# Twelve expert slots in one straight plan, with the rare groups and the fallbacks behind one test each at the end

## The chip, the core and the metric

The kernel runs on one core of a Trainium2 chip. The time of a run is the device time of one execution in microseconds. PE is the matrix engine (TensorE; PEld is its queue of weight loads), DVE is VectorE, ACT is ScalarE, POOL is GpSimd, and SP starts most of the transfers. Each engine works through its instructions in the order in which they were written for it; semaphores make one wait for another.

## The reference

There are 3072 tokens (4 sequences of 768), 384 numbers wide (8 heads of 48). Three layers follow one another.

```python
# 1. a linear recurrence per head, complex decay, real output
a_n = a * min(|a|, 0.999) / (|a| + 1e-6)
S[t] = a_n[t, :, None] * S[t-1] + k[t, :, None] * v[t, None, :]      # 48 x 48, complex
y[t] = q[t] @ S[t].real
# 2. a dense layer with a rational function
h = x @ w_in                                      # 3072 x 384 @ 384 x 2048
g = (a0 + a1 h + a2 h^2 + a3 h^3) / (1 + |b0| |h| + |b1| h^2 + 1e-6)
x = g @ w_out                                     # 2048 x 384
# 3. a mixture: each token goes to one of 8 experts
logits = normalize(x) @ normalize(emb).T / tau
e = argmax(logits); gate = softmax(logits)[e]
out = gate * (relu(x @ w1[e]) @ w2[e])            # 384 x 1024, 1024 x 384
```

All of it is fp32. A product is made of three matmuls of rounded parts (x_hi w_hi + x_lo w_hi + x_hi w_lo), so every operand is split on ACT, DVE or POOL into a high part (a copy, L967) and a low part (a difference, L1387 for expert weights, L1366 for tokens).

## The kernel before

**Order.** Nearly nothing is written in the order in which it runs. A stage hands its operations to a `Plan` with the engines that may do them, their costs, what they read and write and a due time; `Plan.emit` then writes them out one by one by a greedy rule with prices for each engine. Attention has one plan; the rational layer, the routing and the first eight slots share one (knobs `MOE`); each branch behind that has one of its own (knobs `TAIL`). A branch ends a plan: all engines read a flag (L153, L1631) and branch (L154, L1653, L1703).

**Attention** leaves its result in `xT`, transposed; its last pieces come by transfers on SP (L660). Two checks on DVE set `bad`: decays that the fast recurrence can't take, and coefficients that the fast rational function can't take. The branch at L154 holds a slow recurrence and a slow rational layer, which also fills `safe`; with these data it is not taken.

**The rational layer** takes 8 blocks of 384 tokens through 8 units of 256 inner columns: up products (L1003), the function on ACT and DVE (L1026 to L1038), down products (L1048). `route` follows a block: its rows are copied, replaced by rows of `safe` under a condition (`mend`, L1075, 24 transfers on SP), the expert is chosen, tokens are counted (L1103 to L1108) and listed for each expert (L1115, scatters on POOL).

**The mixture** takes slots of 256 tokens of one expert. A slot is gathered on POOL (`gather`, L1343), transposed on PE (L1361), split (L1366), its gates are copied (L1368); its weights are loaded by SP into one raw buffer per matrix (`load`, L1327), and split (`slot_split`). `work` then does four quarters: up products, relu (gh on L1421, gl on L1422; those of quarters 2 and 3 are gh, gl2e, gh3e, gl3e), down products (L1433). The two halves of the slot are scaled by the gate (L1438) and scattered to the output on POOL (L1391). In a slot that ends a stretch (`end`), all up products stand first, then the down products of the first half of the tokens, then those of the second. What slots there are is computed by DVE as chains of small operations on one partition (L978). Tokens left over by full slots go into remainders of 32 (`mini`, L1548 to L1569) beside slots 4 to 7, and into halves of 128 behind the last branch (`halves`).

Eight slots are certain for any routing (`LAST` = 8). For more there are three branches of 4, 2 and 1 slots (L1653), then the branch for halves (L1703). The straight part and each branch also prepare what the next branch needs: slot `hi` wholly (`ready`: gather, load, transposes, splits), of slot `hi + 1` the gather and the load. With these data there are 12 full slots, so the branch of four is taken and the others are not. Where a body ends, POOL has a semaphore instruction that waits for all its transfers (INC_SWDGE_SEM in the rows).

Of the kernel before, what the change touches and what calls it, by code (L numbers as in the profile page):

```python
# [9 lines left out]
F32 = mybir.dt.float32  # L10
# [29 lines left out]
NSURE = (NT - E * HALF) // SLOT - NEARLY  # L40
NTAIL = 7
# [40 lines left out]
def constants():  # L82
# [20 lines left out]
    c[:, C_J:C_J + NSLOT] = list(range(NSURE + 4)) + [NSURE, NSURE + 1, NSURE, NSURE + 1]  # L103
# [15 lines left out]
def tile_recurrence_rational_moe(tc, q, k, v, a_re, a_im, w_in, w_out, ca, cb, emb, tau, w1, w2, cst_d, out):  # L119
# [3 lines left out]
    with ExitStack() as top:  # L123
# [18 lines left out]
        with ExitStack() as moe1:  # L142
            xtp = moe1.enter_context(tc.tile_pool(name="xtp", bufs=1))
            xT = xtp.tile([P, KT, NT], F32, name="xT")
            wfp = moe1.enter_context(tc.tile_pool(name="wfp", bufs=1))
            hold = moe1.enter_context(tc.tile_pool(name="hold", bufs=1))
# [4 lines left out]
            with ExitStack() as att:  # L151
                attention(tc, att, q, k, v, a_re, a_im, w_in, w_out, emb, cst, cst_d, cc, misc, ident, hold, xT, bad, idl, x2d, coef, parts, xs)
            flag = lambda i: nc.values_load(bad[0:1, i:i + 1], min_val=0, max_val=1) != 0  # L153
            with tc.If(flag(0)):  # L154
                with tc.If(flag(1)):
                    sequential_attention(tc, q, k, v, a_re, a_im, cst, cc, ident, dram, xT, coef)
                    for kk in range(KT):
                        xs.hi(nc.scalar, 0, kk)
                        xs.lo(nc.gpsimd, 0, kk)
# [253 lines left out]
def attention(tc, ctx, q, k, v, a_re, a_im, w_in, w_out, emb, cst, cst_d, cc, misc, ident, hold, xT, bad, idl, x2d, coef, parts, xs):  # L413
# [290 lines left out]
    A.preload_act_table_set("trig_and_small")  # L704
    for t in vraw + sraw:
        G.memset(t[:, DM:W], 0.0)
    V.memset(rows[0], 0.0)
    V.memset(gap[:, 2:4, :], -2.0)
    load_a(0, 0)
    load(cst[:, 0:C_ID], cst_d[:, 0:C_ID], ["misc"], 0.1)  # L710
    ext = raw[0].rearrange("p f w -> p (f w)").bitcast(F32)[:, 0:NX * P]
    load(ext, cst_d[:, C_X:C_X + NX * P], [("raw", 0)], 0.92)
    add(("V", 0.41), lambda e: V.tensor_copy(trir, ext.rearrange("p (n m) -> p n m", n=NX)), r=[("raw", 0)], w=["trir"])
    load_a(0, 1)
    load(cst[:, C_ID:], cst_d[:, C_ID:C_N], ["cst"], 1.2)
# [20 lines left out]
    for g in range(NG):  # L736
        u = g // NB
        if g % NB == 0:
            if u:
                for i in range(NB):  # L740
                    load_a(u, i)
        load_q(g)
        if g == 0:
            prep(0, 0)
            prep(0, 1)
        elif g % NB == 0:
            if u in HALVED:
                prep(u, 0)
                prep(u, 1)
            else:  # L750
                prep(u)
        phases(g)
# [12 lines left out]
        chunk(g)  # L765
# [5 lines left out]
    m, mm = new("m", [P, 1])[0], new("mm", [1, 1])[0]  # L771
    top = new("top", [P, 3])[0]

    def worst(i):
        def fn(e):
            V.tensor_reduce(out=top[:, i:i + 1], in_=rows[i], axis=AX.X, op=ALU.max)
            if i:
                V.tensor_scalar(top[:, i:i + 1], top[:, i:i + 1], (-FAR_SQ, MAG_LOW)[i - 1], None, op0=ALU.add)
        add(("V", 0.16), fn, r=[("gap", n, g) for n in range(2) for g in range(NG)], w=[("top", i)])

    for i in range(3):
        worst(i)
    add(("V", 0.1), lambda e: V.tensor_reduce(out=m, in_=top, axis=AX.X, op=ALU.max), r=[("top", i) for i in range(3)], w=["m"])
    add(("T", 0.1), lambda e: T.transpose(pb("pm")[0:1, :P], m, ident), r=["m"], w=["pm"], take=("B", "pm"))
    add(("V", 0.2), lambda e: V.tensor_reduce(out=mm, in_=pb("pm")[0:1, :P], axis=AX.X, op=ALU.max), r=["pm"], w=["mm"], give="pm")
    add(("V", 0.1), lambda e: V.tensor_scalar(bad[0:1, 1:2], mm, 0.0, None, op0=ALU.is_gt), r=["mm"], w=["bad"], due=end)
    add(("V", 0.1), lambda e: V.tensor_copy(bad[0:1, 2:3], coef.flag[0:1, :]), r=["coef"], w=["bad"], due=end)
    add(("V", 0.1), lambda e: V.tensor_tensor(out=bad[0:1, 0:1], in0=bad[0:1, 1:2], in1=bad[0:1, 2:3], op=ALU.max), w=["bad"], due=end)
# [7 lines left out]
    seen = [("xT", i, r) for i in (0, 1) for r in {r for h in range(H) for r in (h * D, (h * D // P + 1) * P)}]  # L796
    for kk in range(KT):
        qs, ks = ([(n, i) for i in range(NQ)] if not kk else [] for n in ("q", "k"))
        add(("A", 0.41), lambda e, kk=kk: xs.hi(A, 0, kk), r=seen + (["x0"] if kk else []), w=qs + ks + ([] if kk else ["x0"]) + [("xh", kk)], due=end)
        add(("G", 0.96), lambda e, kk=kk: xs.lo(G, 0, kk), r=seen + [("xh", kk)], w=[("xl", kk)], due=end)  # L800
# [120 lines left out]
def mixture(tc, ctx, cst, cc, misc, ident, cp, hold, wfp, parts, xs, xT, cnt, idl, x2d, w1, w2, out, coef, bad, safe):  # L921
# [133 lines left out]
    rows, kept = [], []  # L1055
# [7 lines left out]
    def route(b):  # L1063
# [8 lines left out]
        def mend(t):  # L1072
            if not kept:
                kept.append(val(bad[0:1, 2:3], 1))
            SY.dma_start(rows[t], safe[b * BLK + t * P:b * BLK + (t + 1) * P, :], cond=kept[0])  # L1075

# [85 lines left out]
    tail = row("tail", 8, I32)  # L1162
# [34 lines left out]
    ns, ce, nf, tf = row("ns", E), row("ce", E), row("nf", E), row("tf", 4)  # L1197
# [13 lines left out]
    def slot_table(V):  # L1211
# [9 lines left out]
        rest = tf[:, 3:4]  # L1221
        V.tensor_scalar(rest, ce[:, E - 1:E], float(NSURE), None, op0=ALU.subtract)
        groups(V, tf, rest, (4, 2, 1))
        V.tensor_copy(tail[:, 0:3], tf[:, 0:3])
        V.tensor_copy(jb, cst[0:1, C_J:C_J + NSLOT])
        V.tensor_scalar(tf[:, 0:2], tf[:, 0:2], 2.0, None, op0=ALU.mult)
        for n, o in ((0, 4), (0, 4), (1, 6)):
            V.tensor_scalar(jb[:, NSURE + o:], jb[:, NSURE + o:], tf[:, n:n + 1], None, op0=ALU.add)
# [510 lines left out]
```

## Time and profile before

| | us |
|---|---|
| runs (three) | 967.56, 960.59, 961.06; median 961.06 |
| profiled execution | 965.73 |
| its span | 964.0 |
| PE busy in it | 879.6 (91%) |
| DVE, ACT, POOL busy | 747.4, 704.4, 280.8 |

The span is the stretch that the profile records, from the first instruction to the last; the execution is 1.7 us longer. Attention ends near 256 on PE, the rational layer near 690, the straight slots near 860. In the rows below a time in front is microseconds from the span's start, and an arrow in brackets (<-) names what ended the wait before an operation.

### The profile page before, as it was taken

What the parts mean: (1) busy time and instruction counts of PE and PEld (TensorE: products, weight loads), DVE (VectorE), ACT (ScalarE), POOL (GpSimd) and SP (SyncE); (2) the same over time, 40 slices, a digit from 0 to 9 for tenths busy, and PEclk for the clock granted to TensorE, in tenths of its full rate; (3) what the DMA queues carried; (4) which work ended last, traced back from release to release, by engine and by line L of the source; (5) the groups of instructions that cost most, each with busy time, mean ns of one, the idle gap of its engine ahead of it and who ended that gap; (6) DMA issues with size and microseconds to landing.
All of it is one profiled execution on the core that took longest, in us unless ns stands there. A gap on an engine that the chain in (4) does not pass through costs nothing.

```text
span 964.0 us, 17300 instructions
## 1 busy us (share of the span) xinstructions
PE 879.6 (91%) x6125; PEld 835.8 (87%) x6125; DVE 747.4 (78%) x1444; ACT 704.4 (73%) x1133; POOL 280.8 (29%) x213
## 2 busy tenths in 40 slices
PE   2899999989689999999999999999989999999960
PEld 2788897878679999999999999999889888879960
DVE  7989998879799988787978788886986865566250
ACT  7989998969576898888889898978545444345540
POOL 2425444445353110101010010103033234316881
PEclk9999999969889999999999999999999999999985
DMA  9978997764300000000100000105112276631511
GB/s 174 196 171 182 186 186 161 166 142 107 85 1 1 1 1 25 9 18 1 25 1 26 1 25 1 26 1 151 39 27 67 47 217 190 221 118 27 172 39 32
DMA packets 178236, 78.73 MB, mean 82 GB/s; under 512 B 145672, under 2 KB 172184, under 8 KB 178132
## 3 DMA queue, kind: packets, MB, share of 16 engines
q1 hardware_dynamic: 173460, 65.60, 30.1%
q0 software_dynamic: 4672, 11.83, 4.5%
q8 instruction: 55, 0.90, 0.4%
q14 instruction: 49, 0.40, 0.2%
HBM read 105.48 MB, written 9.96 MB: 120 GB/s over the span
## 4 chain that ended last, share of the span: by engine, by line
PE 56%; DVE 6%; ACT 3%; issue 3%; POOL 3%; DMA 0%; POOLq 0%; DVEq 0%; ACTq 0%
PE ph L1003 27%; PE acc L1048 18%; PE acc L1433 8%; POOL wi L1387 1%; DVE xT L978 1%; PE acc L1361 1%; DVE wo L1387 1%; PE ph L1548 1%; DVE sq L1034 1%; DVE u L1036 1%; POOL out_dram L1391 1%; DMA out_dram<-ah,ido 0%; DVE wi L1387 0%; ACT sq L1026 0%; POOL wo L1387 0%
## 5 line engine op out<-in xcount | busy, mean ns | idle before, releaser
L1003 PE MATMUL ph<-xh,wi 128*128 128x384 f32 (+1 forms) x1284 | 305.0, 316 | 10.7 <-DVEq L154 7.6
L1003 PEld LDWEIGHTS ph<-xh,wi 128*128 128x128 f32 x1284 | 223.1, 189 | 14.2 <-issue 10.1
L1048 PE MATMUL acc<-wo,gh 128*128 128x392 f32 x768 | 202.2, 345 | 3.3 <-ACT gh L1037 3.3
L1003 PE MATMUL ph<-xl,wi 128*128 128x384 f32 (+1 forms) x642 | 202.6, 316 | 0.2 <-DVE xl L1366 0.2
L1048 PEld LDWEIGHTS acc<-wo,gh 128*128 128x128 f32 x768 | 141.2, 190 | 3.6 <-ACT gh L1037 3.6
L1048 PE MATMUL acc<-wo,gl 128*128 128x392 f32 x384 | 132.1, 344 | 1.4 <-DVE gl L1038 1.3
L1003 PEld LDWEIGHTS ph<-xl,wi 128*128 128x128 f32 x642 | 121.5, 189 | 0.4 <-DVE xl L1366 0.4
L1115 POOL DMA_INDIRECT idl<-tok,pos x24 | 25.0, 1042 | 304.1 <-DVE pos L1112 152.7
L1048 PEld LDWEIGHTS acc<-wo,gl 128*128 128x128 f32 x384 | 72.9, 190 | 2.4 <-DVE gl L1038 2.3
L1433 PE MATMUL acc<-wo,gh 128*128 128x384 f32 x272 | 71.9, 345 | 0.0
L1421 ACT ACTIVATE gh<-ph 128x512 fp32r<-128x512 f32 x34 | 20.4, 600 | 58.0 <-PE ph L1003 45.6
L1038 DVE TENSOR_TENSOR gl<-u,gh 128x768 fp32r<-128x768 f32 x48 | 46.9, 978 | 19.5 <-PE acc L1048 18.7
L1343 POOL DMA_INDIRECT xT<-x2d,ids x28 | 30.5, 1090 | 103.4 <-DVE oh L1094 43.1
L1026 ACT ACTIVATE sq<-ph,quad 128x768 f32<-128x768 f32 x43 | 38.8, 902 | 26.7 <-PE ph L1003 24.3
L1031 DVE SCALAR_TENSOR_TENSOR u<-u,qtmp,ph 128x768 f32<-128x768 f32 x47 | 47.4, 1009 | 13.2 <-ACT u L1029 12.8
L485 ACT COPY qkT<-bank 96x512 f32<-96x512 f32 x96 | 51.0, 587 | 6.2 <-PE bank L607 5.8
L616 PE MATMUL bank<-qkT 96*128 96x128 f32 x384 | 51.1, 281 | 1.1 <-ACT qkT L485 1.1
L606 PE MATMUL bank<-cst,qf 128*96 128x128 f32 x192 | 49.7, 296 | 2.3 <-ACT qkT L485 2.3
L1034 DVE SCALAR_TENSOR_TENSOR sq<-sq,quad,ah 128x768 f32<-128x768 f32 x43 | 46.2, 1075 | 6.5 <-ACT ah L1033 6.4
L1433 PEld LDWEIGHTS acc<-wo,gh 128*128 128x128 f32 x272 | 48.1, 191 | 2.5 <-issue 1.7
L616 PEld LDWEIGHTS bank<-qkT 96*128 96x128 f32 x384 | 47.5, 195 | 2.5 <-ACT qkT L485 2.3
L1387 DVE TENSOR_TENSOR wo<-xT,wo 128x768 fp32r<-128x768 f32 x41 | 40.8, 1024 | 10.2 <-ACT wo L967 10.1
(308 smaller groups left out, 2195.9 us busy)
## 6 DMA issues: line engine op xcount, KB each, us to landing
xT<-in_moe_w_dram SPq DMA_DIRECT2D x28, 1536.0 KB
mw<-in_moe_w_dram SPq DMA_DIRECT2D x32, 384.0 KB
raw<-in_moe_w_out_dram SPq DMA_DIRECT2D x16, 384.0 KB
raw<-in_moe_w_in_dram SPq DMA_DIRECT2D x16, 384.0 KB
rows<-safe SPq DMA_DIRECT2D x24, 196.0 KB
x2d<-rows SPq DMA_DIRECT2D x24, 192.5 KB
a_re<-in_a_re_dram SPq DMA_DIRECT2D x24, 192.0 KB
a_im<-in_a_im_dram SPq DMA_DIRECT2D x24, 192.0 KB
```

The costliest lines, as they stand in the source:

```text
L485: (A.copy if e == "A" else eng[e].tensor_copy)(o, i)
L606: T.transpose(pv[:, i, 0, :], Q[:, 2 * j + i, :], ident)
L616: T.matmul(pb(b)[:, i * P:(i + 1) * P], O[:, i, 1, :], O[:, i, 0, :], start=True, stop=True)
L1003: T.matmul(o, l, r, start=(n == 0), stop=(n == len(steps) - 1))
L1026: add(("A", 0.81 if many else 0.45), lambda e, c=c, h=h: A.activation(z[:, c], h(), AF.Abs, scale=coef.kb), w=kh + kz_)
L1031: add(("V", 0.93 if many else 0.53), lambda e, c=c, h=h: V.scalar_tensor_tensor(out=w[:, c], in0=w[:, c], scalar=coef.d, in1=h(), op0=ALU. ...
L1034: add(("V", 0.93), lambda e: V.scalar_tensor_tensor(out=z, in0=z, scalar=coef.e, in1=s, op0=ALU.add, op1=ALU.mult), r=ks, w=kz_)
L1038: add(("V", 0.87), lambda e: V.tensor_tensor(out=l, in0=w, in1=g.bitcast(F32), op=ALU.subtract), r=kw + kg, w=kl, lat=0.27)
L1048: T.matmul(o, x[:, j, sl], y("o", i)[:, c], start=(i == 0 and j == 0 and k == 0), stop=(i == NP - 1 and j == 1 and k == 2))
L1343: G.indirect_dma_start(out=xg[i][t], out_offset=None, in_=x2d[0:n, :], in_offset=bass.IndirectOffsetOnAxis(ap=ids[i][:, t:t + 1], axis=0), ...
L1387: add([("V", 0.87)] if lone and k else [("V", 0.87), ("G", 1.76)], lambda e, src=src, v=v, o=o: eng[e].tensor_tensor(out=v(wset(s, q)[o + ...
L1433: T.matmul(o, x[:, j, sl], w[:, c], start=(q == 0 and j == 0 and n == 0), stop=(q == NQ - 1 and j == 1 and n == 2))
```

## The change

`NSURE` goes from 5 to 9, so `LAST` is 12: twelve slots are written in the straight plan, whatever the routing. The groups behind it are of 2 and 1 slots; they and the halves stand together behind one new flag, `tail[8]`, the maximum of the flags of the two groups and of the halves. The branch between attention and mixture is gone. If `bad` is set, a branch at the end of the program holds a second run: the slow recurrence, the slow rational layer and the whole mixture once more. The rows of `safe` are copied in that second run alone, without a condition. `plan_half` (gathers for seven halves in the straight plan) and the preparation of the next branch (`ready`) are gone; of the slot after the last one only the load under a condition stays. The buffers for the weights' parts are numbered anew from slot 8 on, and the last slot, 11, now has the order `end`. The planner's knobs are as they were.

```diff
-NSURE = (NT - E * HALF) // SLOT - NEARLY
-NTAIL = 7
+NSURE = NT // SLOT - NEARLY
+EXTRA = (2, 1)
+NTAIL = sum(EXTRA)
...
-            with tc.If(flag(0)):
-                with tc.If(flag(1)):
-                    sequential_attention(tc, q, k, v, a_re, a_im, cst, cc, ident, dram, xT, coef)
...
-                with tc.If(flag(2)):
-                    plain_rational(tc, coef, parts, xT, safe)
-            mixture(tc, moe1, cst, cc, misc, ident, cp, hold, wfp, parts, xs, xT, cnt, idl, x2d, w1, w2, out, coef, bad, safe)
+            prepare(False)
+            with ExitStack() as first:
+                rare, rest = layers(first, False)
+                with tc.If(nc.values_load(rare, min_val=0, max_val=1) != 0):
+                    rest()
+            with tc.If(nc.values_load(bad[0:1, 0:1], min_val=0, max_val=1) != 0):
+                xs.tiles.clear()
+                prepare(True)
+                sequential_attention(tc, q, k, v, a_re, a_im, cst, cc, ident, dram, xT, coef)
...
+                plain_rational(tc, coef, parts, xT, safe)
+                with ExitStack() as second:
+                    layers(second, True)[1]()
...
-            add(("S", 0.65 if b or t else 2.25), lambda e, t=t: mend(t), w=[("row", t)], lat=1.8)
+            if again:
+                add(("S", 0.65), lambda e, t=t: SY.dma_start(rows[t], safe[b * BLK + t * P:b * BLK + (t + 1) * P, :]), w=[("row", t)], lat=1.8)
...
+        V.tensor_tensor(out=tail[:, 8:9], in0=tail[:, 0:1], in1=tail[:, 1:2], op=ALU.max)
+        V.tensor_tensor(out=tail[:, 8:9], in0=tail[:, 8:9], in1=tail[:, 7:8], op=ALU.max)
...
     def chunk(s, q):
         n = NQ * s + q
-        return n % 6 if NEARLY <= s < LAST else n % 8
+        if s >= LAST:
+            return 2 + n % 6
+        return n % 6 if NEARLY <= s < BESIDE.stop else (n + (2 if s >= BESIDE.stop else 0)) % 8
...
-        work(s)
-        m = s - NEARLY - 1
-        if 0 <= m < NMINI:
+        if s == BESIDE.stop:
+            mini_end()
+        work(s, s == LAST - 1)
+        if s in BESIDE:
+            m = s - BESIDE.start
             mini_load(NHALF + m)
             mini(m, st.start(s) + 5.0)
-        if s == NEARLY + 1:
-            for p in (0, 1, 2, 3, 8, 9, 10):
-                plan_half(p)
-    mini_end()
-    ready(LAST)
-    gather(LAST + 1)
-    load(LAST + 1)
+    load(LAST)
...
-    for n, (lo, hi) in enumerate(((0, 4), (4, 6), (6, 7))):
-        with tc.If(flag(n)):
-            group(LAST + lo, LAST + hi)
...
+    def rest():
+        for n, lo in enumerate((LAST, LAST + EXTRA[0])):
+            with tc.If(flag(n)):
+                group(lo, lo + EXTRA[n])
+        with tc.If(flag(7)):
...
+    return tail[:, 8:9], rest
```

On PE, between the last product of attention (`bank`) and the first up product of the rational layer (`ph`), there stood before:

```order
L634 MATMUL bank_153<-qkT_142,S_138 64x128
L153 TENSOR_LOAD bad
L154 COMPARE_AND_BRANCH
L153 TENSOR_LOAD bad
L155 COMPARE_AND_BRANCH
...
L915 MATMUL pr_acc_3011<-wfo_171,pr_w 128x392
L160 UNCONDITIONAL_BRANCH x2
L154 UNCONDITIONAL_BRANCH
L1003 MATMUL ph_5281<-xh_2619,wi_0_2532 128x384
```

and there stands now:

```order
L646 MATMUL bank_153<-qkT_142,S_138 64x128
L644 MATMUL bank_153<-at_145,v_136 64x128
L646 MATMUL bank_153<-qkT_142,S_138 64x128
L1016 MATMUL ph_2779<-xh_2619,wi_0_2532 128x384
L1016 MATMUL ph_2779<-xl_2620,wi_0_2532 128x384
```

The branch with its body of two fallbacks is gone, and the two layers follow one another.

On DVE, where the tables of the slots are computed (`xT` 1x8, 1x13 and so on are rows of that computation, in a corner of xT's buffer), the chain stood before between the gl of slot 0's second quarter and gl2e of its third:

```order
L1422 SCALAR_TENSOR_TENSOR gl_5277<-ph_5282,gh_5274 128x2x256
L1108 COPY cnt<-acc_5283 128x8
...
L978 TENSOR_SCALAR xT<-cst 1x8
L1366 TENSOR_TENSOR xl_5338<-acc_5286,xh_5337 128x3x128
L978 TENSOR_TENSOR xT<-xT 1x8
...
L978 SCALAR_TENSOR_TENSOR xT<-xT 1x13
L978 TENSOR_SCALAR xT<-xT 1x13 x2
L1366 TENSOR_TENSOR xl_5338<-acc_5285,xh_5337 128x3x128
L1422 SCALAR_TENSOR_TENSOR gl2e<-ph_5281,gh_5275 128x2x256
L1422 SCALAR_TENSOR_TENSOR gl3e<-ph_5282,gh3e 128x2x256
```

and stands now behind gl3e, the last one of slot 0, and in front of slot 1's first gl:

```order
L1447 SCALAR_TENSOR_TENSOR gl2e<-ph_2779,gh_2773 128x2x256
...
L1411 TENSOR_TENSOR wi_1_2980<-xT,wi_0_2895 128x768
...
L1411 TENSOR_TENSOR wi_1_3094<-xT,wi_0_3091 128x768
...
L1447 SCALAR_TENSOR_TENSOR gl3e<-ph_2780,gh3e 128x2x256
L991 TENSOR_SCALAR xT<-cst 1x8
L980 CAST wo_0_3031<-xT 128x768
...
L991 TENSOR_SCALAR xT<-xT 1x13 x2
L1447 SCALAR_TENSOR_TENSOR gl_2774<-ph_2779,gh_2771 128x2x256
L1447 SCALAR_TENSOR_TENSOR gl_2775<-ph_2780,gh_2772 128x2x256
```

On POOL the group of four ended before in weight splits (`wi`, `wo`) and gathers (`xT<-x2d`) between the output scatters (`out_dram`):

```order
L1391 DMA out_dram<-ah_5266,ido_5313 3072x384
L1387 TENSOR_TENSOR wi_1_2592<-xT,wi_0_2569 128x768
L1387 TENSOR_TENSOR wi_1_5344<-xT,wi_0_5335 128x768
L1343 DMA xT<-x2d,ids_5309 128x385 x2
L1391 DMA out_dram<-ah_5267,ido_5314 3072x384 x2
L1653 UNCONDITIONAL_BRANCH
L1653 ISA
L1653 UNCONDITIONAL_BRANCH
L1631 TENSOR_LOAD xT
L1653 COMPARE_AND_BRANCH
```

and now the last stretch of the straight plan has there:

```order
L1411 TENSOR_TENSOR wo_1_2897<-xT,wo_0_2883 128x768
L1415 DMA out_dram<-ah_2764,ido_2809 3072x384
L1411 TENSOR_TENSOR wi_1b<-xT,wi_0b 128x768
L1415 DMA out_dram<-ah_2765,ido_2810 3072x384 x2
L1415 DMA out_dram<-ah_2764,ido_2811 3072x384 x2
L1415 DMA out_dram<-ah_2765,ido_2812 3072x384 x2
L163 TENSOR_LOAD xT
L163 COMPARE_AND_BRANCH
L1636 TENSOR_LOAD xT
```

The last six scatters follow one another, and the new test at L163 stands right behind them.

## Rows read from the trace of the kernel before

**Rows 1.** The page: engine, busy us (share of the span), instructions.
```profile
PE 879.6 (91%) x6125; PEld 835.8 (87%) x6125; DVE 747.4 (78%) x1444; ACT 704.4 (73%) x1133; POOL 280.8 (29%) x213
```

**Rows 2.** Busy time by stretch: from:to, length, busy us per engine (instructions), PEclk, DMA share, GB/s.
```profile
320.00:670.00 350.00, 350.00 (x1996) 349.96 (x1995) 290.50 (x518) 303.81 (x425) 26.82 (x25) 1.00 0.08 21
...
800.00:850.00 50.00, 48.80 (x375) 42.45 (x374) 27.61 (x58) 21.84 (x37) 20.67 (x18) 1.00 0.72 228
863.00:900.00 37.00, 36.85 (x267) 36.82 (x268) 19.83 (x31) 18.33 (x29) 25.22 (x15) 1.00 0.24 71
900.00:930.50 30.50, 30.50 (x216) 30.46 (x215) 8.33 (x14) 14.79 (x23) 26.00 (x18) 1.00 0.34 98
930.50:964.00 33.50, 0.84 (x8) 0.58 (x5) 8.20 (x14) 4.84 (x8) 9.75 (x8) 0.55 0.11 32
```

**Rows 3.** Timeline of PE, last useful matmul: start, us, engine, line, operation.
```profile
930.34 0.34 PE L1433 MATMUL acc<-wo_0b,gl3e 128*128 128x384 f32 x1
```

**Rows 4.** Timeline of DVE and ACT behind it, with idle time before and its releaser.
```profile
932.67 4.03 DVE L1387 TENSOR_TENSOR wo<-xT,wo 128x768 fp32r<-128x768 f32 x1 [8.94 <-ACT wo L967]
...
936.70 0.20 DVE L1368 COPY xT<-xT 128x1 f32<-128x1 f32 x2
...
936.87 1.05 ACT L1438 ACTIVATE ah<-acc,xT 128x384 f32<-128x384 f32 x2 [2.04 <-DVE xT L1368]
```

**Rows 5.** Timeline of POOL, the last two output scatters.
```profile
940.16 1.45 POOL L1391 DMA_INDIRECT out_dram<-ah,ido  x1 [0.30 <-issue]
945.40 1.00 POOL L1391 DMA_INDIRECT out_dram<-ah,ido  x1 [3.79 <-DMA out_dram<-ah,ido]
```

**Rows 6.** Lines L1653, L1703, L1734 on POOL's queue: ns min/median/max, first to last start.
```profile
L1653 POOLq INC_SWDGE_SEM  x2: 1853/1866/1879, 948.6 to 951.4; - x2
...
L1703 POOLq INC_SWDGE_SEM  x1: 1843/1843/1843, 954.2 to 954.2; - x1
...
L1734 POOLq DRAIN  x3: 40/107/7019, 956.1 to 963.7; - x3
```

**Rows 7.** Output scatters of the whole run, from issue to landing.
```profile
DMA to landing us min/median/max: 2.5/3.0/7.2
```

**Rows 8.** Timeline of PE at the first boundary.
```profile
263.03 0.66 PE L1003 MATMUL ph<-xh,wi 128*128 128x384 f32 x1 [7.56 <-DVEq L154]
```

**Rows 9.** Timeline of DVE at the first boundary.
```profile
259.03 0.55 DVE L476 SCALAR_TENSOR_TENSOR wfi<-wa,bank 128x384 f32<-128x384 f32 x1
265.54 0.07 DVE L1060 MEMSET seen<- 128x8 f32 x1 [5.95 <-DMA xT<-y]
...
271.57 1.01 DVE L1031 SCALAR_TENSOR_TENSOR u<-u,qtmp,ph 128x768 f32<-128x768 f32 x1 [0.63 <-ACT u L1029]
...
273.92 2.17 DVE L1034 SCALAR_TENSOR_TENSOR sq<-sq,quad,ah 128x768 f32<-128x768 f32 x1 [0.39 <-ACT ah L1033]
```

**Rows 10.** Line L154, the branches of POOL and of PE's weight queue.
```profile
L154 POOLq COMPARE_BRANCH  x1: 45/45/45, 256.7 to 256.7; - x1
L154 PEldq COMPARE_BRANCH  x1: 3447/3447/3447, 256.7 to 256.7; - x1
```

**Rows 11.** Timeline of PE at the entrance of the four slots.
```profile
859.68 0.83 PE L1566 MATMUL ph<-rows,cst 128*32 128x384 f32 x2 [0.62 <-ACT rows L967]
...
863.15 0.38 PE L1003 MATMUL ph<-xh,wi 128*128 128x256 f32 x1 [0.31 <-DVE rows L1569]
```

**Rows 12.** Timeline of PE in slot 0.
```profile
708.71 0.69 PE L1433 MATMUL acc<-wo,gl2e 128*128 128x384 f32 x1 [3.36 <-DVE gl2e L1422]
```

**Rows 13.** Timeline of DVE in slot 0, the chain's first operation and what follows it.
```profile
698.30 0.15 DVE L978 TENSOR_SCALAR xT<-cst 1x8 f32<-1x8 f32 x1
...
707.98 0.67 DVE L1422 SCALAR_TENSOR_TENSOR gl2e<-ph,gh 128x512 fp32r<-128x512 f32 x1
```

**Rows 14.** The page's costliest groups: weight splits of the slots on DVE (busy, mean ns).
```profile
L1387 DVE TENSOR_TENSOR wo<-xT,wo 128x768 fp32r<-128x768 f32 x41 | 40.8, 1024 | 10.2 <-ACT wo L967 10.1
```

**Rows 15.** Line L1075, the conditional copies on SP's queue.
```profile
L1075 SPq DMA_DIRECT2D rows<-safe x24: 73/88/112, 336.6 to 691.5; - x24
```

More of the change, by code (lines that the diff above doesn't have):

```diff
@@ L702, in weight @@
             plan.ops[-1].due = due
[L704 to L715, printed above, removed]
+    if not again:
+        A.preload_act_table_set("trig_and_small")
+        for t in vraw + sraw:
+            G.memset(t[:, DM:W], 0.0)
+        V.memset(rows[0], 0.0)
+        V.memset(gap[:, 2:4, :], -2.0)
+        load_a(0, 0)
+        load(cst[:, 0:C_ID], cst_d[:, 0:C_ID], ["misc"], 0.1)
+        ext = raw[0].rearrange("p f w -> p (f w)").bitcast(F32)[:, 0:NX * P]
+        load(ext, cst_d[:, C_X:C_X + NX * P], [("raw", 0)], 0.92)
+        add(("V", 0.41), lambda e: V.tensor_copy(trir, ext.rearrange("p (n m) -> p n m", n=NX)), r=[("raw", 0)], w=["trir"])
+        load_a(0, 1)
+        load(cst[:, C_ID:], cst_d[:, C_ID:C_N], ["cst"], 1.2)
     def embed(e):
@@ L737, in attention @@
         u = g // NB
[L738 to L752, printed above, removed]
+        if not again:
+            if g % NB == 0:
+                if u:
+                    for i in range(NB):
+                        load_a(u, i)
+            load_q(g)
+            if g == 0:
+                prep(0, 0)
+                prep(0, 1)
+            elif g % NB == 0:
+                if u in HALVED:
+                    prep(u, 0)
+                    prep(u, 1)
+                else:
+                    prep(u)
+            phases(g)
         if g == 0:
@@ L770, in attention @@
     end = STEP * NG
[L771 to L787, printed above, removed]
@@ L1070, in spread @@
             return rows
[L1072 to L1075, printed above, removed]
         over = [("wf", NF - 2), ("wf", NF - 1)] if not b else []
@@ L1311, in mixture @@
     LAST = NEARLY + NSURE
-    turn4 = lambda s: 0 if s == LAST + NTAIL - 1 else s % 4
+    turn4 = lambda s: s % 4
+    BESIDE = range(NEARLY + 1, NEARLY + 1 + NMINI)
     def cols(s):
@@ L1378, in wset, with slot_split @@
         return c(wh("i", n)), c(wl("i", n)), c(wh("o", n)), c(wl("o", n))
-    def slot_split(s, q, lone=False):
+    def slot_split(s, q):
         n = chunk(s, q)
+        anew = s >= BESIDE.stop and n >= 6 and n not in renewed
+        renewed.update([n] if anew else [])
         v1 = lambda t: t.rearrange("p (k f) -> p k f", k=KT)
@@ L1441, in work @@
             add(("G", 1.04), lambda e, t=t: scatter_out(ido[turn4(s)][:, t:t + 1], ah[i][:, t, :], P), r=[("ah", i, t), ("ido", turn4(s))], w=["out"], lat=1.9, dma=0.55, due=base + GROUP + 10.0)
-    def ready(s, wait=0.0):
-        gather(s)
-        load(s)
-        trans(s, wait)
-        for q in range(NQ):
-            slot_split(s, q, wait > 0)
     hx = [t.rearrange("p a b -> p (a b)")[:, 0:XC] for t in sq + u] + [room(P, XC) for _ in range(2)]
@@ L1660, in mixture @@
     hw = [t.rearrange("p (k f) -> p k f", k=KT) for t in hw[:NQ]], [t.rearrange("p (f d) -> p f d", f=2) for t in hw[NQ:]]
-    held = [raw1[:, :, q * SLOT:(q + 1) * SLOT] for q in range(NQ)], [raw2[:, 2 * q:2 * q + 2, :] for q in range(NQ)]
     def half_load(p, cond):
```

153 lines of the change are left out of this document (81 added, 72 removed).

## The prediction

> **What bounds the kernel now.** I read the busy times first: TensorE (PE) works 879.6 us of a span of 964.0 [rows 1], so only the stretches in which it stands still are to be had. The table of stretches says where they are [rows 2]. From 320 to 670 (the rational layer) PE is busy for the whole 350.00 us. From 800 to 850, among the expert slots of the straight part, it lacks 1.20 us in 50. In the four slots that the branch adds (863 to 930.5) it lacks 0.15 us in 67.5. From 930.5 to the end it works 0.84 us in 33.5. So the kernel is bound by PE up to its last useful matmul and by something else behind it.
>
> That last matmul ends at 930.34 + 0.34 = 930.7 [rows 3]; call this T. The end lies 33.3 us later, and the reader should follow it through four engines. VectorE (DVE) and ScalarE (ACT) are still splitting the weights of slot 12, which no token needs: the split at 932.67 takes 4.03 us, and behind it, in DVE's order, stand the two gate copies at 936.70 for which the last scaling by the gate waits on ACT; that starts only at 936.87 [rows 4]. POOL is held up in the same way: the last two output scatters start at 940.16 and 945.40, the second after 3.79 us of waiting for an earlier scatter to land [rows 5]. At 948.6 POOL leaves the branch body, passes two groups that are not taken and the flag of the remainders (a semaphore instruction of 1.84 to 1.88 us at 948.6, 951.4 and 954.2), and drains for 7.02 us from 956.1 [rows 6].
>
> **The change, part by part.** (a) **The end.** Slots 8 to 11 are now written straight, and nothing of a slot 12 is gathered, transposed or split; its weights are still asked for under a condition. What is left behind T is worked out so. The last half of the last slot is scaled on ACT: two such operations take 1.05 us together [rows 4], so one takes about 0.6, with 0.2 for the handing over: the last scatter starts at T + 0.8. The one before it doesn't hold it up: by the order the first half's sums are complete 24 matmuls ahead of T, which at 30.50 us for 216 matmuls [rows 2] is 3.4 us. From a scatter's start to the semaphore instruction took 948.6 - 945.40 = 3.2 us, so the first such instruction stands at T + 4.0. From there to the end took 964.0 - 948.6 = 15.4 us with three of them; now there are two (one for the rare groups, one for the second run), and one round was 951.4 - 948.6 = 2.8 us. So the end is T + 4.0 + 12.6 = T + 16.6, a gain of 33.3 - 16.6 = **16.7**. Best case: a landing of 2.5 instead of 3.2 [rows 7], 17.4. Worst case: the last scatter waits for the one before it as it did, 5.2 us from start to start, which from T - 3.4 + 0.8 is T + 2.6 in place of T + 0.8, 1.8 us more, and each of the two branches costs what a far one cost elsewhere (below), 6.8 more: 8.1.
>
> (b) **The branch between attention and mixture** goes. PE's first product waited 7.56 us there and started at 263.03 when DVE came through L154 [rows 8]; DVE's last operation before it ended at 259.03 + 0.55 = 259.6 [rows 9], so PE may start 3.4 us earlier. That isn't the gain, since the ramp behind it hangs on DVE: its first operation at 265.54 waits for the transposed copies of attention's result (xT<-y), which stay, and then its weight casts run without a gap. What an earlier PE and ACT give back is only DVE's idle time for ACT, 0.63 us at 271.57 and 0.39 at 273.92 [rows 9]. I take **1.0**; the ends are 0 and 3.4.
>
> (c) **The branch in front of the four slots** goes. PE lost 0.62 us there on the last remainder's row copy and 0.31 a little later [rows 11]. In the new order matmuls of the next slot stand in between, and I take the whole **0.9**; the other end is 0.
>
> (d) **The tables of the slots.** DVE computed them from 698.30 on as a chain of 47 small operations, in front of gl2e of slot 0 at 707.98, and PE stood 3.36 us for it [rows 12, 13]. In the new order 43 of them stand behind gl3e of slot 0 and in front of slot 1's first gl, while PE has 68 matmuls to do: 12 of slot 0, three times 18 up products and two down. The chain lasted 9.7 us with two other operations of 0.54 in it, 8.6 without them, 7.9 for 43; with a cast of 0.55 and the gl of 0.67 that is 9.1 us on DVE against 68 x 0.141 = 9.6 on PE. That is covered, barely. Ahead of it gl3e now stands behind two weight splits of 1.02 [rows 14], one operation of 0.54 and eleven small ones of about 0.17, with itself 5.1 us, where PE has some 30 matmuls, 4.2 us: a new stall of 0.9. I take 3.4 - 0.9 = **2.5**. The ends are 3.4, and a loss of 3.7 if slot 1's up products come late, so that only 14 matmuls (2.0 us) cover the 9.1 and 7.1 are lost instead of 3.4.
>
> (e) **One plan for all twelve slots.** The four last slots had a plan with prices of their own and a PE that lacked nothing; the plan of the others let it lack 1.20 in 50. At that rate 67.5 us lose 1.6. Part of the 1.20 belongs to the remainders that run beside slots 4 to 7 only, so I take the middle, a **loss of 0.8**; the ends are 0 and 1.6.
>
> (f) **At nothing:** the 24 conditional copies on SP (mend, 0.09 us each from 336.6 to 691.5 [rows 15]) and the seven gathers for halves. Most of the copies lie between 320 and 670, where PE lacked nothing; the last block's three stand ahead of the counting and so of the chain in (d), where their going can only help. The gathers were on POOL, which works 280.8 us in all [rows 1], and nobody read what they fetched. The scatters of the last block's token lists now stand behind two weight splits and a gather on POOL; what hides them is that the tables, which the late slots need as well, are not ready sooner. If that cover were gone it would cost what stands ahead of them, some 5 us, once.
>
> Sum: -16.7 - 1.0 - 0.9 - 2.5 + 0.8 = -20.3. The profiled execution took 965.73 us, so it would become 945.4. It lies 4.7 above the median of the runs shown, 961.06, and nothing in the terms depends on that, so the same difference from the median gives **940.8 us**. With the likelier ends (0.7 and 1.8 in the tail, 1 in (b), 1.5 in (d), 0.8 in (e)) this case alone reaches from 937 to 946.
>
> **Rivals.** *Far branches cost at the end as they did at the first boundary.* At L154 PE's weight queue took 3.447 us for the branch, POOL 0.045 [rows 10]. The end hangs on POOL, whose branches over groups of some hundred matmuls cost it nothing that the rows show; this speaks against. But the two new ones pass far more code, all rare groups and a whole second run. At 3.4 each, 6.8 us: 947.6. The Trainium skill states this as a rule (Runtime: NRT & Kernel Launch, Instruction fetch mechanics): a taken branch whose target isn't in the pages at hand must wait for a DMA to fetch the target's page. By that rule POOL would pay twice, and the time is this rival's; the trace agrees on PE and not on POOL.
>
> *The slots gain as well.* If the new plan loses nothing anywhere, the 1.20 per 50 us between 680 and 863 (4.4), the 0.9 of (d) and the 0.8 of (e) come back too, and with 2.4 more in (b) that is 8.5: 932.3. For it speaks only that the order is another; the plan's prices are the old ones.
>
> *Slower: weights of slots 8 to 11 come late.* There is one raw buffer for each of the two weight matrices, and a slot's load can't start before the last split of the slot ahead has read it. In these slots POOL now does 7 splits instead of 26 (some of those were for slot 12), and DVE takes the rest: 19 x 1.02 = 19.4 us on top of the 28.2 busy us of 67.5 [rows 2, 14]. That fits, which speaks against, but DVE works in order: where a split waits for its load, the gl that PE needs is behind it. If a slot comes to wait for a whole load, 1536 KB at 228 GB/s [rows 2] is 6.9 us, and with one split 7.9. Four slots lose 31.6 us: 971.6, 1.1% above the median. It decides against the change from 20.3 us on, 5.1 a slot; half of it leaves about 956, no difference to speak of.
>
> *The change doesn't do what it says*: the rare flag is set by these data, and a group runs behind it. Before, both later groups were passed over within 2.8 us each [rows 6], so twelve slots are enough; next to nothing.
>
> **How the numbers follow.** A measurement of this kernel tells about 1%, 9.6 us, from no change. Forecast 0.65 (faster), slots gain too 0.10 (faster), far branches 0.13 (faster, 947.6 against 951.5), late weights by half 0.07 (same), late weights in full or the wrong path 0.05 (slower). With a little moved from the first to the middle for terms that I don't see: faster 0.86, same 0.08, slower 0.06. The range takes in both neighbours and leaves the late weights out: 932 to 950.
>
> **What would show it.** After the last useful matmul: no split, one round of scatters, two semaphore instructions instead of three, about 16.6 us to the end. At the first boundary PE starts near 259.6 while DVE still starts near 265.5. Near 700 a stall of less than 1 us in place of 3.36. In the last four slots PE idle of 1 to 2 us. The forecast is wrong if PE waits in slots 8 to 11 for weight splits, if POOL's branch at the end takes microseconds, or if the chain of tables moves its stall instead of losing it.

## The result, and the profile after

The changed kernel is faster, by about half of what was forecast. In four runs beside four of the kernel before, its median is 951.75 us against 962.76; the ratio of the two is 0.988 (95% interval 0.984 to 0.992). Once more on another chip (e6) it was 950.52 against 960.61, ratio 0.990 (0.988 to 0.992). So 10 to 11 us went where 20 were forecast, and the measured time lies outside the range.

The profiled execution took 952.94 us, its span is 951.2. The table by stretch (columns as in [rows 2]) shows where PE now stands still:

```profile
700.00:710.00 10.00, 10.00 (x80) 10.00 (x79) 7.61 (x46) 4.60 (x9) 3.94 (x4) 1.00 0.08 20
710.00:750.00 40.00, 34.69 (x231) 33.83 (x229) 30.19 (x94) 18.84 (x31) 8.83 (x8) 0.96 0.19 51
750.00:800.00 50.00, 44.19 (x312) 39.52 (x313) 34.73 (x84) 22.84 (x39) 18.83 (x15) 0.93 0.57 168
800.00:850.00 50.00, 49.31 (x388) 42.18 (x387) 28.19 (x43) 24.08 (x41) 10.87 (x9) 1.00 0.56 178
...
863.00:900.00 37.00, 37.00 (x271) 36.93 (x270) 22.10 (x35) 21.69 (x34) 19.67 (x13) 1.00 0.36 122
900.00:930.50 30.50, 30.50 (x215) 30.36 (x213) 6.61 (x10) 6.80 (x12) 3.88 (x4) 1.00 0.10 34
930.50:952.00 21.50, 0.21 (x2) 0.00 (x0) 0.00 (x0) 0.58 (x1) 0.97 (x1) 0.59 0.06 15
```

Before, the same stretches of slots 0 to 4 were:

```profile
700.00:710.00 10.00, 6.64 (x41) 6.32 (x40) 8.89 (x44) 4.42 (x7) 1.97 (x2) 0.92 0.03 1
710.00:750.00 40.00, 39.01 (x273) 38.50 (x272) 29.09 (x79) 18.68 (x31) 14.38 (x11) 0.98 0.20 56
750.00:800.00 50.00, 48.48 (x357) 44.54 (x356) 37.33 (x96) 21.56 (x37) 14.47 (x14) 1.00 0.52 144
```

Read the first table from below. From 930.5 to the end of the span, 951.2, it is 20.7 us instead of 33.5. The four last slots keep PE busy to the last digit; before, they lacked 0.15 us. But between 710 and 800, in slots 1 to 4, PE lacks 11.1 us of 90 where it lacked 2.5 before (and 3.4 between 700 and 710), and the granted clock falls to 0.96 and 0.93 there. PE's timeline names the waits; the first line is the first boundary, which answers to [rows 8], and the second answers to [rows 12]:

```profile
253.84 0.69 PE L1016 MATMUL ph<-xh,wi 128*128 128x384 f32 x1 [4.18 <-DVE wfi L488]
...
715.01 0.44 PE L1458 MATMUL acc<-wo,gh 128*128 128x384 f32 x1 [3.42 <-DVE wo L1411]
...
774.68 0.52 PE L1373 MATMUL acc<-cst,xT 128*128 128x128 f32 x3 [1.87 <-ACT xh L980]
779.06 0.87 PE L1545 MATMUL acc<-cst,rows 128*128 128x128 f32 x3 [3.86 <-DMA rows<-x2d,hids]
...
856.14 0.83 PE L1578 MATMUL ph<-rows,cst 128*32 128x384 f32 x2 [0.36 <-ACT gh3e L1446]
```

The wait for the tables, 3.36 us for gl2e, is gone, and one of 3.42 us for a weight split (wo) stands in slot 1. A wait of 3.86 us at the transposes of the remainders, in this execution for their gathered rows, is new.

At the end, ACT's two scalings by the gate start 0.03 us after T = 930.72 and, for the first half, 4.2 us ahead of it; POOL's scatters answer to [rows 5]:

```profile
927.42 0.97 POOL L1415 DMA_INDIRECT out_dram<-ah,ido  x1 [5.17 <-ACT ah L1463]
932.68 0.97 POOL L1415 DMA_INDIRECT out_dram<-ah,ido  x1 [4.29 <-DMA out_dram<-ah,ido]
```

The second still waits for the first to land. POOL's queue behind it (branch, then semaphore instruction, at each of the two tests, then the drain) answers to [rows 6]:

```profile
L163 POOLq COMPARE_BRANCH  x1: 53/53/53, 933.1 to 933.1; - x1
L163 POOLq INC_SWDGE_SEM  x1: 1668/1668/1668, 937.4 to 937.4; - x1
...
L165 POOLq COMPARE_BRANCH  x1: 50/50/50, 939.5 to 939.5; - x1
L165 POOLq EVENT_SEMAPHORE  x6: 17/30/43, 942.0 to 942.4; - x6
L165 POOLq INC_SWDGE_SEM  x1: 1641/1641/1641, 942.5 to 942.5; - x1
...
L1736 POOLq DRAIN  x3: 40/107/6117, 944.2 to 950.9; - x3
```

A branch instruction itself takes 0.05 us, but behind the second one 3.0 us pass until the semaphore instruction, 2.4 of them before POOL's next instruction of any kind (942.0). In [rows 6] it is 2.8 us from one semaphore instruction to the next in all.

### The profile page after: what moved, and what is told of

Same layout as the page of the kernel before. It is cut to its first block, busy times and chain, and to the rows that moved or that the text cites. A ratio compares the mean times of both kernels' runs of the same rounds, so it can differ in the third digit from the quotient of the medians.

```text
span 951.2 us, 16898 instructions
## 1 busy us (share of the span) xinstructions
PE 876.5 (92%) x6119; PEld 832.3 (88%) x6119; DVE 738.4 (78%) x1418; ACT 704.6 (74%) x1134; POOL 239.5 (25%) x184
## 5 line engine op out<-in xcount | busy, mean ns | idle before, releaser
L1061 PEld LDWEIGHTS acc<-wo,gh 128*128 128x128 f32 x768 | 141.1, 189 | 4.4 <-ACT gh L1050 4.4
L1446 ACT ACTIVATE gh<-ph 128x512 fp32r<-128x512 f32 x36 | 21.6, 599 | 48.7 <-PE ph L1016 33.4
L1415 POOL DMA_INDIRECT out_dram<-ah,ido x24 | 29.8, 1242 | 98.0 <-ACT ah L1463 54.9
L1458 PEld LDWEIGHTS acc<-wo,gh 128*128 128x128 f32 x256 | 45.8, 194 | 9.4 <-issue 4.9
L1355 POOL DMA_INDIRECT xT<-x2d,ids x24 | 27.2, 1133 | 98.2 <-DVE oh L1102 45.9
```

What stands on the lines that cost most here:

```text
L1061: T.matmul(o, x[:, j, sl], y("o", i)[:, c], start=(i == 0 and j == 0 and k == 0), stop=(i == NP - 1 and j == 1 and k == 2))
L1355: G.indirect_dma_start(out=xg[i][t], out_offset=None, in_=x2d[0:n, :], in_offset=bass.IndirectOffsetOnAxis(ap=ids[i][:, t:t + 1], axis=0), ...
L1415: G.indirect_dma_start(out=out[:, :], out_offset=bass.IndirectOffsetOnAxis(ap=dst, axis=0), in_=src, in_offset=None, bounds_check=NT - 1, ...
L1458: T.matmul(o, x[:, j, sl], w[:, c], start=(q == 0 and j == 0 and n == 0), stop=(q == NQ - 1 and j == 1 and n == 2))
```

## The experiments

For each profile the execution was cut at three points: attention's last matmul, the first product of the rational layer, and T, the end of the last useful matmul. "Gap" is what lies between the first two, "stretch" from the second to T, with PE's waits in the ramp (the first 62 us) and later; "end" is from T to the end of the span.

| kernel | median / before beside it | gap | stretch | waits: ramp, later | end |
|---|---|---|---|---|---|
| before | 962.8 | 7.6 | 667.7 | 6.5, 9.4 | 33.3 |
| changed | 951.8 / 962.8 | 4.2 | 676.9 | 8.5, 13.7 | 20.5 |
| e1 two plans | 957.2 / 968.4 | 4.2 | 680.9 | 9.2, 16.6 | 24.2 |
| e2 no branches at the end | 941.6 / 968.4 | 4.2 | 677.6 | 8.3, 15.1 | 8.8 |
| e3 before, front branch out | 964.9 / 968.4 | 4.2 | 677.9 | 8.6, 14.7 | 33.4 |
| e4 before, only the end | 950.0 / 968.4 | 7.3 | 678.4 | 7.2, 15.0 | 15.6 |
| e5 before again | 963.1 / 960.6 | 7.4 | 669.6 | 6.5, 10.8 | 32.8 |
| e6 changed again | 950.5 / 960.6 | 4.2 | 674.7 | 8.6, 13.1 | 20.3 |
| e7 mixed chain | 947.6 / 960.6 | 4.2 | 671.8 | 8.5, 10.9 | 20.8 |
| e8 remainder weights once | 951.7 / 960.6 | 4.2 | 675.5 | 8.3, 12.2 | 20.6 |
| e9 e7 and rows late | 943.4 / 968.6 | 4.2 | 666.6 | 8.9, 6.6 | 20.3 |
| e10 one branch | 950.4 / 968.6 | 4.2 | 680.7 | 8.2, 16.5 | 14.4 |
| e11 all three | 937.3 / 968.6 | 4.2 | 664.1 | 7.3, 6.3 | 14.4 |

e1 to e4 shared a chip, e5 to e8 another, e9 to e11 a third; before itself takes 960.6 to 968.6 from chip to chip, so times are compared on one chip.

**e1, two plans.** The order of slots 8 to 11 is planned by itself again, without a branch (SPLIT is 8).

```diff
-    for s in range(LAST):
+    SPLIT = BESIDE.stop
+    for s in range(SPLIT):
...
-    load(LAST)
+    mini_end()
+    gather(SPLIT)
+    load(SPLIT)
+    trans(SPLIT)
...
+    st.plan, st.delay = Plan({"C": range(4)}, TAIL), T_DELAY
+    for s in range(SPLIT, LAST):
...
+        work(s, s == LAST - 1)
```

> The changed kernel with the order of slots 0 to 11 planned as before: slots 0 to 7 and the preparation of 8 and 9 in the first plan, slots 8 to 11 in a plan of their own with the prices of the groups, but no branch between them; both branches at the end stay. Theory A (one plan for twelve slots costs PE): from the first product of the rational layer to the last useful matmul the changed kernel took 676.9 us and the kernel before 667.7; with two plans it goes back to 668 to 670, and the time to about 943 to 945. Theory B (the plan is innocent; the stretch is longer because the ramp starts at another moment, or by chance of one execution): the time stays at 950 to 953.

The ratio to before is 0.988 (0.981 to 0.994), no better than the changed kernel's. The stretch is 680.9 us against 677.6 in e2, which has the changed kernel's order on the same chip. Its waits are the same ones (5.59 us for wo, 5.04 at the remainders' transposes). Between 863 and 920 PE is busy in both, but for 0.17 us in e1. Theory A falls as it was put: that slots 8 to 11 stand in the common plan costs nothing.

**e2, no branches at the end.** The rare groups, the halves and the second run are left out.

```diff
-                with tc.If(nc.values_load(rare, min_val=0, max_val=1) != 0):
-                    rest()
-            with tc.If(nc.values_load(bad[0:1, 0:1], min_val=0, max_val=1) != 0):
...
-                    layers(second, True)[1]()
```

> The changed kernel without the rare groups, halves and second run and without their two branches. Theory C (POOL pays for far branches): from the last scatter to the end 18.5 us become about 11 (3.2 landing, 6 to 7 drain, 1 events), since each branch cost a semaphore instruction of 1.65, a load and 1.5 to 2.5 of waiting for code: 7 to 8 us less, about 944. Theory D (the branches themselves cost little, only the two semaphore instructions go): 3.5 to 4 us less, about 948.

The end goes from 20.3 to 20.5 us in the changed kernel to 8.8, more than either theory had. POOL's last scatters and its queue at the end show why:

```profile
924.47 0.97 POOL L1403 DMA_INDIRECT out_dram<-ah,ido  x1 [5.17 <-ACT ah L1451]
928.66 0.97 POOL L1403 DMA_INDIRECT out_dram<-ah,ido  x1 [3.22 <-ACT ah L1451]
```

```profile
L1724 POOLq EVENT_SEMAPHORE  x4: 17/17/17, 935.8 to 936.5; - x4
L1724 POOLq DRAIN  x3: 45/107/7322, 928.4 to 936.3; - x3
```

The last scatter starts at T + 0.9 and waits for ACT alone, and the drain of 7.3 us begins at 928.4, beside it. In the changed kernel, with the branches behind the scatters, POOL first waits until everything has landed, then the semaphore instruction comes twice, and the drain only after that (944.2). So the two branches cost 11.5 to 11.7 us together: theory C in kind, with the drain on top.

**e3, the front branch alone.** The branch goes from the kernel before, with its two fallbacks.

```diff
-            with tc.If(flag(0)):
-                with tc.If(flag(1)):
...
-                    plain_rational(tc, coef, parts, xT, safe)
```

> The kernel before without the branch between attention and mixture (its two fallbacks are left out), all else as it was. PE's wait at the boundary goes from 7.6 to about 4.2 as in the changed kernel. If the ramp gives the rest back, 1 to 2 us less than before (0.998 to 0.999); if the 3.4 us stay gained, 0.9965; if the ramp eats all, no difference.

The ratio is 0.996 (0.994 to 0.999). The gap is 4.18 us, as in the changed kernel, and the ramp's waits are 8.6 us against 7.2 in e4, which has the branch and shares the chip; so 3.1 come in and 1.4 go back. By the interval the whole is 1 to 6 us, which doesn't tell 1.7 from 3.4.

**e4, the end alone.** In the kernel before the four slots stand straight in their plan, with no preparation of slots 12 and 13 and nothing behind them.

```diff
-        if hi < LAST + NTAIL:
-            ready(hi, STAY)
-            gather(hi + 1)
-            load(hi + 1)
...
-    for n, (lo, hi) in enumerate(((0, 4), (4, 6), (6, 7))):
-        with tc.If(flag(n)):
-            group(LAST + lo, LAST + hi)
+    group(LAST, LAST + 4)
...
```

> The kernel before with the group of four written straight in its own plan, without the preparation of slots 12 and 13 and with nothing behind it (groups of 2 and 1 and halves left out); the branch between attention and mixture stays. The slots then keep the stretch they had, and only the end changes: from the last useful matmul to the end 33.3 us become 2 to the last scatter, 3.2 landing, 7 drain, 1 events = 13: 20 us less, about 942. If the order of the slots suffers when the preparation goes, less than 16 us are gained.

The end is 15.6 us, 17.7 less than before, and the ratio 0.980 (0.974 to 0.987): 18.4 us between the medians. The forecast of 13 missed because the last four scatters all stand around and behind T: the gate copies and indices that they need stand on DVE behind the last gl (at 931.4 and later), the first starts at 932.40, and each of the others waits for the landing of the one before it, 3.3 to 3.4 us apart; the last one starts 7.1 us behind T. That the end alone gives what it takes away from the end, without loss elsewhere, puts the missing gain of the changed kernel on its new order and on its branches.

**e5 and e6, both kernels again.** Unchanged copies.

> The kernel before once more, for a second profile of it. Theory E (the profile that the prediction was made from was one of two kinds): the stretch from the first product of the rational layer to the last useful matmul takes 677 to 679 us, as with the same order in the two experiments made from it (677.9 and 678.4), and not the 667.7 of that profile; attention ends near 248 to 250 instead of 255.5. Theory A (the plan for twelve slots lengthened the stretch): 667 to 669 again.

> The changed kernel once more, timed beside the kernel before. The ratio should be 0.985 to 0.990 again. In the profile the stretch takes 676 to 678 us, the boundary 4.2, the end 20 to 21 us, of which the part behind the last scatter is 18 to 19.

Theory E fell on this chip: before's stretch is 669.6 us there, near the 667.7 of the first profile; the 678 of e3 and e4 belong to their chip. Side by side, from e5 to e6: gap -3.2, ramp +2.0, later waits +2.3, PE's own work +0.8, end -12.5. The sum is -10.6 us, and the medians differ by 10.1. Where attention ends varies from execution to execution (246 to 255 us, with the branch and without), and it isn't part of this sum.

**e7, the mixed chain.** The tables of the slots are due later and with less haste.

```diff
-            chain(calls(slot_table), "tb", r=["cnt"], last=[("tab", 2)], due=st.start(3) - 20.0, rush=0.2)
+            chain(calls(slot_table), "tb", r=["cnt"], last=[("tab", 2)], due=st.start(3) - 12.0, rush=0.15)
```

> The changed kernel with the chain of the tables due 8 us later and at a lower rank of haste, so that it no longer stands as one block on DVE: the weight split that slot 1 needs first (wo of its first quarter) now stands behind two operations of the chain instead of behind all 43 and four gl. Theory F (the block of small operations holds up what is behind it, whichever it is): PE's stall of 3.4 us near 715 (for wo) goes to below 1, and no new one of that size comes between 690 and 740; 2.5 to 3.5 us less. Theory G (the wait is for ACT or for the load of the weights): it stays above 2.5.

The median is 947.55 us against 950.52 of e6 on the same chip, 3.0 less, and the stall is gone: no wait of PE between 690 and 760 is above 0.73 us. DVE's timelines show the difference. First the changed kernel, from the chain's end on:

```profile
708.50 0.24 DVE L991 TENSOR_SCALAR xT<-xT 1x13 int32<-1x13 f32 x2
709.99 0.69 DVE L1447 SCALAR_TENSOR_TENSOR gl<-ph,gh 128x512 fp32r<-128x512 f32 x1 [1.25 <-ACT gh L1446]
711.46 0.69 DVE L1447 SCALAR_TENSOR_TENSOR gl<-ph,gh 128x512 fp32r<-128x512 f32 x1 [0.78 <-PE ph L1016]
712.06 0.68 DVE L1447 SCALAR_TENSOR_TENSOR gl2e<-ph,gh 128x512 fp32r<-128x512 f32 x1
713.40 0.69 DVE L1447 SCALAR_TENSOR_TENSOR gl3e<-ph,gh3e 128x512 fp32r<-128x512 f32 x1 [0.66 <-ACT gh3e L1446]
714.01 0.95 DVE L1411 TENSOR_TENSOR wo<-xT,wo 128x768 fp32r<-128x768 f32 x1
```

Then e7, from slot 0's last gl on (the chain's small operations left out):

```profile
694.83 0.69 DVE L1447 SCALAR_TENSOR_TENSOR gl3e<-ph,gh3e 128x512 fp32r<-128x512 f32 x1 [0.52 <-ACT gh3e L1446]
...
696.16 0.94 DVE L1411 TENSOR_TENSOR wo<-xT,wo 128x768 fp32r<-128x768 f32 x1
...
699.26 0.94 DVE L1411 TENSOR_TENSOR wo<-xT,wo 128x768 fp32r<-128x768 f32 x1
...
701.09 0.67 DVE L1447 SCALAR_TENSOR_TENSOR gl<-ph,gh 128x512 fp32r<-128x512 f32 x1
```

What PE waits for at 715 isn't the gl that the prediction looked at. It is the split of wo, which stands behind the chain and behind all four gl, of which two wait for ACT and one for PE's products. In e7 that split (at 696.16) and the next one stand ahead of the first gl. Theory F holds.

**e8, the remainders' weights once.**

```diff
-            mini_load(NHALF + m)
+            if not m:
+                mini_load(NHALF + m)
```

> The changed kernel with the weights of the remainders loaded for the first one alone (8 transfers of 384 KB instead of 32; the other three remainders are computed with the first one's weights, which leaves out part of the computation's data). Theory H (the loads crowd the transfers that PE waits for, the gathered rows of the remainders above all): PE's waits between 760 and 860, 6.8 us in the changed kernel and 7 to 9 in the experiments, fall below 2. Theory I (the order alone makes them): they stay at 5 or more.

Behind 760 PE still waits 0.75 us and then, at the remainders' transposes, 4.47, 5.2 in all against 6.0 in e6. That is theory I's number, but the edit doesn't test the loads around that wait: the first remainder's eight loads stay, they start between 763.5 and 772.1, and the gather of the rows starts at 770.77. From the gather's start to the transposes the queue of the loads moved 1.9 MB in e8 as in e6. What e8 excludes is the later traffic alone (between 800 and 850, 28 GB/s against 158). Whether the loads make the rows late stays open.

**e9, the rows of the remainders late.** Added to e7:

```diff
-        add(("G", 1.04), mini_rows, r=["mid"] + x2k(NBLK), w=[("row", 0)], lat=1.9, dma=0.55)
+        add(("G", 1.04), mini_rows, r=["mid"] + x2k(NBLK), w=[("row", 0)], lat=15.0, dma=0.55)
```

> The kernel with the mixed chain, and the planner told that the gathered rows of the remainders land after 15 us instead of 1.9, so that their transposes stand some 30 matmuls later on PE. Theory J (PE reaches these transposes before the rows are there, because the planner believes in a short landing): the wait of 4 to 6 us at 770 to 780 goes, 3 to 5 us less than with the mixed chain alone, about 943 to 944 where before is 960.6. Theory K (the rows are late because POOL or DVE are late, and a later place on PE moves the chain behind it too): the wait shows up at the remainders' next steps, and the time stays.

The ratio is 0.973 (0.971 to 0.976). In e7 the gather started at 762.16 and PE reached the transposes too early:

```profile
770.05 0.87 PE L1545 MATMUL acc<-cst,rows 128*128 128x128 f32 x3 [5.71 <-DMA rows<-x2d,hids]
```

In e9 the gather starts at 760.62, and the same instruction waits for nothing:

```profile
778.89 0.49 PE L1545 MATMUL acc<-cst,rows 128*128 128x128 f32 x3
```

The stretch is 666.6 us. On the same chip e10, with the changed kernel's order, takes 680.7, and its later waits are 16.5 us against 6.6; both e7's edit and this one are in that difference. Nothing new stands at the remainders' next steps, so theory K falls. With 7.9 us from the gather's start to PE's (770.05 - 762.16), a planner that reckons with 1.9 puts the transposes too early, as theory J says.

The rows aren't all that PE was too early for, though. The transposes also wait for a split of tokens on DVE (xl), and in e6 that came last, 0.3 us behind the landing of the rows:

```profile
775.03 0.90 PE L1545 MATMUL acc<-cst,rows 128*128 128x128 f32 x3 [4.98 <-DVE xl L1378]
```

In e1, e2, e8 and e10 it is xl as well, 0.1 to 0.5 us behind the landing; in the changed kernel's first profile and in e7 the landing came last, by 0.4 and 0.2. So rows that land sooner would by these traces have saved 0.4 us at most. What e9 shows is that the place of the transposes in PE's order makes the wait; that the landing alone makes it isn't shown.

**e10, one branch at the end.** The flag takes in the checks as well, and behind it stands the whole second run, which is right for any routing.

```diff
+        V.tensor_tensor(out=tail[:, 8:9], in0=tail[:, 8:9], in1=bad[0:1, 0:1], op=ALU.max)
...
-                rare, rest = layers(first, False)
-                with tc.If(nc.values_load(rare, min_val=0, max_val=1) != 0):
-                    rest()
-            with tc.If(nc.values_load(bad[0:1, 0:1], min_val=0, max_val=1) != 0):
+                rare, _ = layers(first, False)
+            with tc.If(nc.values_load(rare, min_val=0, max_val=1) != 0):
```

> The changed kernel with one branch at the end instead of two: one flag for rare groups, halves and the fast paths' checks together, and behind it the whole second run in its slow form. From the last useful matmul to the end 20.3 us should become 20.3 - 5.4 = 14.9, since the second round from semaphore instruction to semaphore instruction took 938.7 - 933.3 = 5.4 us (theory C, each branch is paid on POOL). If the wait is for landings and the drain alone, one branch costs nearly as much as two: 18 or more.

The end is 14.4 us. With 8.8 for no branch and 20.3 to 20.8 for two, a branch there costs 5.6 to 6.4 us, each. The ratio to before is 0.982 (0.980 to 0.985).

**e11, all three.** The edits of e7, e9 and e10 together.

> The changed kernel with the mixed chain, the later place of the remainders' transposes and one branch at the end. If the three are independent: 3.0 + 4 + 5.4 = 12 us less than the changed kernel, about 938 where before is 960.6, a ratio to before of 0.977.

The ratio is 0.969 (0.966 to 0.972), 31 us between the medians, better than forecast. On this chip the edits of e7 and e9 took 14 us from the stretch (680.7 in e10 to 666.6 in e9), where 7 were reckoned from the other chip. This version beats both kernels. Its price lies elsewhere: routing that needs a thirteenth slot or halves now pays for the whole second run.

## Why the prediction was wrong, point by point

Three terms failed: (d) in its mechanism, (e) in its place, and (a), the largest, in its size.

**(a) The end: right in kind, mis-sized.** Forecast 16.7, measured 12.8 (33.3 to 20.5) and 12.5 in the second pair. Two steps failed, both at the value taken and both inside what was named as the worst case. "The one before it doesn't hold it up": it did, the last scatter started at T + 2.0 instead of T + 0.8, since the one before took 4.5 us to land (927.42 to 931.91) where e2, without branches, had 2.6. While it was under way, two blocks of instructions (8 and 16 KB, at 928.6 and 929.0) moved on the instruction queues, and none did in e2; whether they slowed it wasn't tried. And the two rounds on POOL were priced by [rows 6] at 2.8 us each: from the scatter to the first semaphore instruction it took 4.7 instead of 3.2, from there to the second 5.1 instead of 2.8; the rest was 1.1 shorter. 1.2 + 1.5 + 2.3 - 1.1 = 3.9.

So the rival of the far branches, at 0.13, was half true. Behind the branch at L163 POOL's next instruction came 3.7 us later, at 936.9, but the last scatter landed only at 937.2, 4.5 us from its start. The 1.5 us of the first step are thus the landing's as much as the branch's. Behind L165 nothing was left to land, and 2.4 us passed; the 2.3 of the second step are the branch's. Nothing of it is in the branch instruction, which still takes 0.05. The rows of before had misled here: behind their branches (L1653, L1703) POOL's next instruction came 0.1 to 0.4 us later. The new branches pass more code; that this makes the difference wasn't tried by itself. By the Trainium skill (Runtime: NRT & Kernel Launch, Instruction fetch mechanics) a taken branch to a page that isn't at hand waits for it to be fetched. The trace agrees: in the 2.4 us behind L165's branch a block of 8 KB moves on the instruction queue, at 940.5. What the prediction had no term for at all is that the last drain, 7.3 us, could have run beside the last landings if no branch stood there (e2).

**(b) The front: right in size.** Forecast 1.0; the gap gave 3.4 and the ramp's waits took 2.0 back, 1.4 (1.2 in the second pair). That DVE was the limit there is only half borne out: from e5 to e6 PE's waits in the ramp grew for DVE from 3.2 to 4.3 and for ACT (gh) from 3.3 to 4.1.

**(c) The entrance of the four slots: nearly right.** 0.93 became 0.36, a gain of 0.6 for 0.9.

**(d) The tables: wrong in the mechanism.** "That is covered, barely" was true of the gl that the step followed, but the weight split behind the four gl was late instead: 3.36 us became 3.42, a gain of nothing where 2.5 were forecast. The rule in the text (where a stall goes, say what is late next) was kept for gl3e and not for the next splits in DVE's order. e7 shows it: once the split stands ahead, the 3.4 us are gone and nothing takes their place.

**(e) One plan for twelve slots: wrong in place.** Slots 8 to 11 lose nothing (37.00 of 37.00, 30.50 of 30.50), and planning them apart gains nothing (e1). The loss fell on slots 1 to 4, whose order I had compared only around the tables: the remainders' transposes moved ahead of their rows. Before, PE waited 0.2 us for them in the first profile and 1.54 in e5; in the changed kernel 3.86 and 4.98. In the first pair PE came to them 7.3 us behind the gather's start before and 4.2 us in the changed kernel, while the rows took 7.4 and 8.0 us to land. So the landing was as long before, and the place is what changed; e9, with a later place, has no wait. (That DVE's xl was late by as much is said under e9.) In these stretches PE's clock is lower (0.93 between 750 and 800, where it was 1.00 before; a mix of its two levels, 1.2 and 2.4 GHz), and PE's own work over the whole stretch is 0.8 us longer in the second pair and 2.9 in the first. How much of that is the clock wasn't taken apart.

**The slower rival** (late weights in slots 8 to 11) didn't come; POOL's fewer splits there did no harm.

In the second pair the forecast and the measured value differ by 9.7 us: 4.2 from the end, 2.5 from (d), the other 3.0 mainly from (e): it reckoned with a loss of 0.8, and the wait at the remainders' transposes alone grew by 3.4 (1.54 to 4.98).

## What to carry to other kernels

A conditional block that is never entered wasn't free at the end of this program: the last transfers landed before anything else went on, at 5.6 to 6.4 us for each block. So put everything rare behind one flag, and price it by the landing and the drain that it keeps from overlapping. Where an instruction order is written anew, follow what stands behind a moved block on its in-order engine until nothing late is left, and look at every place where PE waits for a gather, not only at the places that the edit names. A greedy planner is as good as its latencies: reckoning with 1.9 us for a landing that took 7 to 9, it put the transposes where PE stood 4 to 6 us for them, and told of 15 us it put them where PE didn't wait.

## What the runs showed that was not expected

- The closing drain on POOL (6.1 to 7.9 us) ran beside the landing of the last scatter where it stood right behind it (e2: starts at 928.4, the scatter at 928.66; e4: 942.2 and 942.40). Ends of 8.8, 14.4 and 20.5 us with no, one and two branches are nearly a straight line.
- Small transfers can land late: the remainders' gather took 6.8 to 8.8 us from its start to its landing in nine profiles (7.2 to 8.9 to PE's use of the rows where that wait is over 1.5 us), with loads of weights beside it. The last two scatters of e2, with nothing beside them, took 2.6. That the loads make the difference wasn't tried.
- The same order took 669.6 us from the first product to the last on one chip and 677.9 to 678.4 in the experiments from it on another, with the same waits at other sizes: PE's wait for a remainder's second product (L1552 and its like) was 0.47 us on the first and 3.7 to 4.2 on the other. Why the chips differ wasn't tried.
